# State and output of a chunked recurrence: two products of 40 and 64 columns per head joined into one of 104

## The chip, the cores and the metric

One core of one Trainium2 chip runs the whole program. The metric is device time in microseconds (us), the median of several executions; lower is better. PE below is TensorE, DVE VectorE, ACT ScalarE, POOL GpSimd, SP SyncE, which only issues transfers here.

## What is computed

The reference is a recurrence over 768 tokens for 4 batches of 8 heads of width 40, followed by two dense layers. Cut to the part that the change touches:

```python
for t in range(S):
    y[:, :, t] = np.einsum('bhd,bhde->bhe', rt, state)
    Sa = np.einsum('bhde,bhe->bhd', state, at)
    state_decay = state * wt[:, :, None, :] - np.einsum('bhd,bhe->bhde', Sa, bt)
    state = state_decay + np.einsum('bhd,bhe->bhde', vt, kt)
...
x = _moe_ref(x=y in token order, **moe_kwargs)   # 320 -> 2048 -> 320, with a sigmoid gate
return _moe2_ref(x=x, **moe2_kwargs)              # 320 -> 2 x 1536 -> 320, silu(gate) * value
```

## The kernel before

The recurrence is cut into 12 steps of 64 tokens (n = 0 to 11). Per step, `prepare` makes decays, scaled keys and a triangular inverse (`late`, from step 5 on, as 62 small DVE operations; `pieces` before that), and `advance` carries the state on. All 32 batch-heads are worked at once: 16 slots i, each holding two heads in partition halves. Products of 64 by 64 use one quarter of PE's array each; the loops run over k, r and p so that four neighbours in the program use four different quarters.

In `advance`, `w_one` and `w_two` make w from v, nk and the state `mt`; `u_mm` turns w into u (copied by ACT in `u_out`). Then:

- State: `m_one` (L1098, `tok0` times `v`) and `m_two` (`tok1` times `u`), 32 products of 40 columns each, summed in a PSUM bank; DVE adds the old state (`m_add`) and scales it (`m_scale`). `d_mm` transposes the state into `md`.
- Output: `ut_mm` transposes u; `scores` (L1227) makes `sv` from `vt` and `r`, and `su` from `ut` and `r`, masked by DVE. `y_old` (L1161) applies the old state in two phases with a drain between, `y_one` and `y_mm` (L1175) add `tok0` times `sv` and `tok1` times `su`, 32 products of 64 columns each. `y_out` scales the result, and `give` sends it by DMA to `xm`, from which the dense layer's input is built.

So `tok0` and `tok1` are each loaded as weights twice per step, once for 40 columns and once for 64.

The first dense layer (`Up`) runs between the pieces of the recurrence: 96 parts h (L495, 8 products of 512 columns, 2 steps of input per 16 parts) and 96 parts o (L522 to L529). The class `Plan` sets the order of everything on every engine at build time: each task has a cost, a due time, data it reads and writes; the recurrence has early due times, the dense parts the last (1e6). Where PE would stand without work, where too little work stood in a stretch before, or where a block of 256 PE instructions would be entered too early, the planner puts in fillers, `warm` (L453, one product of 512 columns of zeros, here called h<-still). The order is fixed; an engine that waits for one task holds all that stands behind it. After the last step the rest of the dense layer runs alone (the tail), then the second layer (`Down`).

```python
        if n + 1 < NT:
            plan.add("PE", 2.6 if 0 < n < self.EARLY else 1.25, m_one, ("v", "tok0", "mt"), ("m.p",), due + 0.005, bank=bm,
            plan.add("PE", 1.25, m_two, ("u", "tok1"), ("m.p",), due + 0.02, bank=bm, work=2200)
```

Of the kernel before, what the change touches and what calls it, by code (L numbers as in the profile page):

```python
# [6 lines left out]
F32 = mybir.dt.float32  # L7
# [5 lines left out]
ALU = mybir.AluOpType  # L13
# [4 lines left out]
B, H, S, D = 4, 8, 768, 40  # L18
DM = H * D
NSTEP = 6  # L20
T = 64
# [551 lines left out]
class Attention:  # L573
# [3 lines left out]
    def __init__(self, tc, ctx, cst, src, up):  # L577
# [32 lines left out]
        self.w = one.tile([128, 16, D], F32, name="w")  # L610
        self.u = one.tile([128, 16, T], F32, name="u")
        self.sv = one.tile([128, 2, H, T], F32, name="sv")
        self.su = one.tile([128, 2, H, T], F32, name="su")
        self.mt = one.tile([104, 2, 4, 2, T], F32, name="mt")
# [19 lines left out]
        v.memset(self.cend, 1.0)  # L634
        nc.gpsimd.memset(self.u, 0.0)
        nc.gpsimd.memset(self.mt, 0.0)
# [20 lines left out]
    def prepare(self, plan, n, due):  # L657
# [365 lines left out]
    def advance(self, plan, n, due):  # L1023

        nc = self.nc
        a, c = self.a[n % 2], self.c[n % 2]
# [32 lines left out]
        plan.add(("ACT",), (0.74,), w_out, ("w.p",), ("w",), due, bank=bw)  # L1059

        def u_mm():
# [9 lines left out]
        def u_out(e):  # L1071
            self.copy(e, self.u.rearrange("q (r k) d -> q r k d", r=2)[:, :, :, 0:D],
                      self.ps[bu.slot][:, :, 0:8 * D].rearrange("q r (k d) -> q r k d", d=D))

        tt = ("ttl", "tt0", "tt0.0", "tt1")
        middle = plan.add("PE", 1.25, u_mm, ("w",) + tt, ("u.p",), due + 0.01, bank=bu, into=("u",))
        plan.add(("ACT",), (0.74,), u_out, ("u.p",), ("u",), due + 0.01, bank=bu)

        def ut_mm():
            ps = self.ps[bx.slot]  # L1080
            for h in range(H):
                nc.tensor.transpose(
                    ps[:, h // 4, 128 * (h % 4):128 * (h % 4) + 128], self.u[:, 2 * h:2 * h + 2].rearrange("q z d -> q (z d)"), self.ident
                )
# [29 lines left out]
        def m_two():  # L1114
            m_part(1, self.u[:, :, 0:D])

# [16 lines left out]

        if n + 1 < NT:
            plan.add("PE", 2.6 if 0 < n < self.EARLY else 1.25, m_one, ("v", "tok0", "mt"), ("m.p",), due + 0.005, bank=bm,
                     work=4300 if 0 < n < self.EARLY else 2200, after=(middle,),
                     size=137 if 0 < n < self.EARLY else 128, real=2.5 if 0 < n < self.EARLY else 1.1)
            plan.add("PE", 1.25, m_two, ("u", "tok1"), ("m.p",), due + 0.02, bank=bm, work=2200)
# [5 lines left out]
        plan.add("PE", 0.9, ut_mm, ("u",), ("ut.p",), due + 0.03, bank=bx, into=("ut",))  # L1144
        plan.add(("ACT",), (1.05,), ut_out, ("ut.p",), ("ut",), due + 0.03, bank=bx)

        for src, dst, keys, d in ((self.vt, self.sv, ("vt", "sv"), -0.2), (self.ut, self.su, ("ut", "su"), 0.04)):
            marks = self.scores(plan, src, dst, keys, due + d)

        by = self.bank()  # L1150
# [15 lines left out]
        def y_part(j, x):  # L1166
            ps = self.ps[by.slot]
            l = self.tok[j].rearrange("q i e -> q (i e)")
            for k in range(8):
                for r in range(2):  # L1170
                    for p in range(2):
                        g, z = divmod(k, 2)
                        o, m = D * (8 * r + k), D if r else 64
                        s = slice(64 * p, 64 * p + 64)
                        nc.tensor.matmul(  # L1175
                            ps[64 * r:64 * r + m, p, T * k:T * k + T], l[s, o:o + m], x[s, z, 4 * r + g],
                            start=(n == 0 and j == 0 and k == 0), stop=(j == 1), skip_group_check=True,
                        )
# [12 lines left out]
        def y_out():  # L1191
            x = self.su[0:104].rearrange("q z h t -> q (z h t)").rearrange("q (k p t) -> q p k t", k=8, p=2)
# [5 lines left out]
        plan.add("PE", 1.25, y_one, ("tok0", "sv"), ("y.p",), due + 0.045, bank=by, work=2100, after=(marks,))  # L1198
        plan.add("PE", 1.25, y_mm, ("tok1", "su"), ("y.p",), due + 0.05, bank=by, into=("su",),
                 work=2500)  # L1200
        plan.add("DVE", 1.26, y_out, ("y.p", ck), ("su",), due + 0.05, bank=by, port=False)

# [15 lines left out]
    def scores(self, plan, src, dst, keys, due):  # L1218
# [13 lines left out]
        def out():  # L1232
            nc.vector.tensor_tensor(
                dst.rearrange("q z h t -> q (z h) t"), self.ps[b.slot].rearrange("q z (h t) -> q (z h) t", t=T),
                self.mask.unsqueeze(1).to_broadcast([128, 16, T]), op=ALU.mult,
            )
# [5 lines left out]
    def give(self, plan, n, due):  # L1242

        nc, t = self.nc, self.xm
        x = self.su.rearrange("q z h t -> q (z h t)").rearrange("q (g c) -> q g c", g=4)
        moves = []
# [6 lines left out]
        for i, (o, s, k) in enumerate(moves):  # L1253
            e, q, cost = ("ACT", nc.scalar, 0.76) if k == "xm1" else ("SP", nc.sync, 0.5)
            plan.add(e, cost, lambda o=o, s=s, q=q: q.dma_start(out=o, in_=s), ("su",), (f"{k}.{i}",), due, kb=80)
        m, half = divmod(n, 2)
# [585 lines left out]
```

## Time and profile before

| | us |
|---|---|
| median of 3 executions | 1117.69 |
| lowest, highest | 1112.75, 1117.75 |
| the profiled execution | 1112.34 |
| its span, first to last instruction | 1110.5 |
| PE busy in the span | 1073.1 (97%) |
| DVE busy | 702.2 (63%) |
| ACT busy | 436.0 (39%) |

In the profile a row of the timeline has a start, a duration from the first start to the last end, the engine, the line, the operation and a count. A 32-bit product of the program is two matrix instructions in the trace, so 32 products read x64. Durations of neighbours on PE overlap, so what a group costs is the start of the next group less its own start.

### The profile page before, as it was taken

To read this page: it belongs to the slowest core of one execution; us is meant where nothing else is said; L and a number is where in the kernel's file an instruction comes from. 1 tells how busy PE (TensorE), PEld (TensorE's weight loads), DVE (VectorE), ACT (ScalarE), POOL (GpSimd) and SP (SyncE) were. 2 spreads that over 40 slices of the span, in tenths; PEclk is the share of its full clock that TensorE was granted. 3 is DMA by queue.
4 is the path that set the end of the run, shared out by engine and by line. 5 is a ranking of instruction groups with operands and counts; after the bars stand their busy time and mean duration, and the time that the engine had idled before them with its cause. 6 is when DMAs were issued, how large, how long until landed. Compare 5 with 4: busy or idle time off the path is not lost.

```text
span 1110.5 us, 38519 instructions
## 1 busy us (share of the span) xinstructions
PE 1073.1 (97%) x16682; PEld 892.6 (80%) x16682; DVE 702.2 (63%) x1406; ACT 436.0 (39%) x814; POOL 98.2 (9%) x115
## 2 busy tenths in 40 slices
PE   8999999899999999999999999999999999999987
PEld 7777777678778787888788878888888888888876
DVE  8976797989697887979653667643443343443221
ACT  3443646454343534344343656432222222222221
POOL 0131123320100000000000323210000000000000
PEclk9896999999999999999999999999999999999999
DMA  6265547664353543544224677430423434341000
GB/s 209 73 184 171 180 150 219 180 195 140 113 166 111 161 133 103 162 127 137 87 62 131 201 212 228 142 90 1 141 69 115 124 116 126 96 147 59 24 1 27
DMA packets 141011, 141.88 MB, mean 128 GB/s; under 512 B 16032, under 2 KB 131744, under 8 KB 140832
## 3 DMA queue, kind: packets, MB, share of 16 engines
q1 hardware_dynamic: 134784, 131.48, 39.1%
q10 hardware_dynamic: 6048, 7.86, 2.1%
q8 instruction: 132, 2.16, 0.8%
q14 instruction: 47, 0.39, 0.1%
HBM read 118.04 MB, written 13.11 MB: 118 GB/s over the span
## 4 chain that ended last, share of the span: by engine, by line
PE 87%; DVE 5%; issue 3%; DMA 2%; ACT 1%; SPq 1%; ACTq 0%; POOL 0%; DVEq 0%
PE gv L1456 24%; PE h L495 15%; PE sums L527 4%; PE oacc L1477 4%; PE oacc L1476 4%; PE oacc L1475 4%; PE sums L528 3%; PE sums L529 3%; PE h L453 3%; PE ps L1175 2%; PE sums L523 2%; PE ps L1098 2%; PE sums L522 2%; PE ps L1227 2%; PE ps L740 1%
## 5 line engine op out<-in xcount | busy, mean ns | idle before, releaser
L1456 PE MATMUL gv<-xst,wg 128*128 128x512 f32 x1152 | 279.9, 395 | 0.0
L1456 PEld LDWEIGHTS gv<-xst,wg 128*128 128x128 f32 x1152 | 213.4, 188 | 45.7
L495 PE MATMUL h<-xst,wi 120*128 120x512 f32 x768 | 197.1, 398 | 0.0
L1461 DVE TENSOR_TENSOR sg<-gv,sg 128x512 f32<-128x512 f32 x72 | 49.8, 692 | 186.5 <-PE gv L1456 184.4
L495 PEld LDWEIGHTS h<-xst,wi 120*128 120x128 f32 x768 | 140.5, 188 | 30.6
L503 ACT ACTIVATE sg<-h 128x512 f32<-128x512 f32 x96 | 57.2, 596 | 152.6 <-PE h L495 145.0
L1462 ACT ACTIVATE gh<-sg 128x512 fp32r<-128x512 f32 x72 | 45.5, 632 | 143.0 <-DVE sg L1461 143.0
L510 DVE TENSOR_TENSOR gl<-sg,gh 128x512 fp32r<-128x512 f32 x90 | 63.4, 704 | 60.2 <-ACT gh L509 60.0
L1460 ACT ACTIVATE sg<-gv 128x512 f32<-128x512 f32 x72 | 43.0, 597 | 136.6 <-PE gv L1456 136.6
L323 POOL TENSOR_TENSOR cvw<-cvu,cva 128x256 uint32<-128x256 uint32 (+2 forms) x89 | 71.6, 805 | 274.1 <-DVE cvu L315 168.5
L1476 PE MATMUL oacc<-wo,gh 128*128 128x320 f32 x288 | 89.0, 309 | 0.0
L1477 PE MATMUL oacc<-wo,gl 128*128 128x320 f32 x288 | 89.0, 309 | 0.0
L1475 PE MATMUL oacc<-wo,gh 128*128 128x320 f32 x288 | 89.0, 309 | 0.0
L527 PE MATMUL sums<-gh,wo 128*128 128x512 f32 x192 | 80.8, 421 | 2.9 <-DVE sg L557 2.6
L1463 DVE TENSOR_TENSOR gl<-sg,gh 128x512 fp32r<-128x512 f32 x72 | 49.9, 692 | 50.2 <-ACT gh L1462 50.2
L528 PE MATMUL sums<-gh,wo 128*128 128x512 f32 x192 | 75.5, 393 | 0.0
L529 PE MATMUL sums<-gl,wo 128*128 128x512 f32 x192 | 75.2, 392 | 0.0
L509 ACT ACTIVATE gh<-sg 128x512 fp32r<-128x512 f32 x96 | 60.7, 632 | 3.6 <-ACT sg L503 0.3
L788 DVE TENSOR_TENSOR tsol<-tsol,tmp 128x126 f32<-128x126 f32 (+22 forms) x217 | 56.3, 260 | 6.7
L780 DVE TENSOR_TENSOR tmp<-tsol,nsol 128x126 f32<-128x126 f32 (+22 forms) x217 | 55.8, 257 | 6.9
L453 PE MATMUL h<-still 128*128 128x512 f32 x183 | 58.3, 466 | 1.1 <-DVE still L412 1.1
L1476 PEld LDWEIGHTS oacc<-wo,gh 128*128 128x128 f32 x288 | 54.1, 188 | 3.2
(182 smaller groups left out, 1618.8 us busy)
## 6 DMA issues: line engine op xcount, KB each, us to landing
wo<-w_out SPq DMA_DIRECT2D x192, 160.0 KB
cva<-out SPq DMA_DIRECT2D x128, 128.0 KB
cva<-gv SPq DMA_DIRECT2D x96, 128.0 KB
kb<-kba SPq DMA_DIRECT2D x92, 104.0 KB
cva<-in_ab SPq DMA_DIRECT2D x64, 120.0 KB
r<-rT SPq DMA_DIRECT2D x48, 104.0 KB
vt<-vT SPq DMA_DIRECT2D x48, 104.0 KB
a<-kba SPq DMA_DIRECT2D x46, 104.0 KB
```

Of the source, the lines that this page charges most:

```text
L323: nc.gpsimd.tensor_tensor(w.bitcast(U32), u, lo, op=ALU.add)
L453: self.nc.tensor.matmul(self.ph[0], c.to_broadcast([128, 128]), c.to_broadcast([128, 512]), start=True, stop=True)
L495: nc.tensor.matmul(ps[:, 0:n], self.wi[:, b, 128 * f:128 * f + 128], x[:, a], start=(e == 0), stop=(e == 7))
L509: add("ACT", 0.63, lambda: nc.scalar.activation(out=hi, in_=sg, func=ACTF.Copy), (f"sg{s}",), (f"gh{d}",))
L510: add(("DVE", "POOL"), (0.74, 1.35), lambda e: self.engine(e).tensor_tensor(lo, sg, hi.bitcast(F32), op=ALU.subtract), (f"sg{s}", f"gh{d}" ...
L527: nc.tensor.matmul(acc[k], w[:, c:c + 128], hi, start=st, stop=False)
L528: nc.tensor.matmul(acc[k], w[:, 256 + c:384 + c], hi, start=False, stop=False)
L529: nc.tensor.matmul(acc[k], w[:, c:c + 128], lo, start=False, stop=sp)
L1456: nc.tensor.matmul(ps, w[:, b], x[:, a], start=(i == 0), stop=(i == 7))
L1475: nc.tensor.matmul(acc[k], hi[:, c], self.wo[:, f, 0], start=st, stop=False)
L1476: nc.tensor.matmul(acc[k], hi[:, c], self.wo[:, f, 1], start=False, stop=False)
L1477: nc.tensor.matmul(acc[k], lo[:, c], self.wo[:, f, 0], start=False, stop=sp)
```

## The change

From step 5 on (`paired`), the state and the output of one head share a product. `v` and `sv` become the two parts of one tile `vs` (16 slots of 40 + 64 columns), `u` and `su` those of `us`. One product of 104 columns with `tok0` or `tok1` then gives both results. Because 104 columns times 8 slots don't fit a bank, the work is done in two halves f of four slots, each in a bank of its own: `pair_old` (the old state's share, with a drain in each half), `pair_mm` with `vs`, `pair_mm` with `us`, then `pair_add` and `pair_out` by DVE, and one `m_scale`. In step 11, which has no next state, only the 64 columns are computed. Before step 5 the products stay apart.

With it go: u is copied by ACT first into `nk` (read by the transposes and, before step 5, by `m_two`), and from step 5 on a second time into `us`; so nk of the next step can't be written before these readers are done. The output is written to `utr` in place of `su`. The mask of `scores` writes rows 104 apart. The load of v writes 40 columns of each 104, in pieces of 160 bytes in place of 640.

```diff
-        self.v = one.tile([128, 16, D], F32, name="v")
+        self.vs = one.tile([128, 16, D + T], F32, name="vs")
+        self.us = one.tile([128, 16, D + T], F32, name="us")
...
+        self.v, self.u = self.vs[:, :, 0:D], self.us[:, :, 0:D]
+        self.sv, self.su = self.vs[:, :, D:D + T], self.us[:, :, D:D + T]
...
-        load(self.v.rearrange("q i d -> q (i d)"), self.vtok[n], "v", 328, 0.6)
+        load(self.v, self.vtok[n].rearrange("q (i d) -> q i d", d=D), "v", 328, 0.6)
...
+        middle = plan.add("PE", 1.25, u_mm, ("w",) + tt, ("u.p",), due + 0.01, bank=bu, into=("nk",))
+        plan.add(("ACT",), (0.74,), lambda e: u_out(e, False), ("u.p",), ("nk",), due + 0.01, bank=bu)
+        if paired:
+            plan.add(("ACT",), (0.74,), lambda e: u_out(e, True), ("u.p",), ("u",), due + 0.01, bank=bu)
...
-        if n + 1 < NT:
+        if not paired and n + 1 < NT:
...
+        def pair_old(b, f):
+            ps = self.ps[b.slot]
+            md = self.md.rearrange("q i r e -> q (i r e)")
+            for ph in (1, 0):
+                if not ph:
+                    nc.tensor.drain()
+                for g in (2 * f, 2 * f + 1):
...
+        def pair_mm(b, f, j, x):
+            ps = self.ps[b.slot]
+            l = self.tok[j].rearrange("q i e -> q (i e)")
+            c = 0 if n + 1 < NT else D
+            for k in range(4):
+                for r in range(2):
+                    for p in range(2):
+                        i = 8 * r + 4 * f + k
+                        s, m = slice(64 * p, 64 * p + 64), D if r else 64
+                        nc.tensor.matmul(
+                            ps[64 * r:64 * r + m, p, W * k + c:W * k + W], l[s, D * i:D * i + m], x[s, i, c:W],
+                            start=False, stop=(j == 1), skip_group_check=True,
+                        )
...
+        if paired:
+            for f in range(2):
+                b = self.bank()
+                yk = (f"y.p{f}",)
+                plan.add("PE", 0.8, lambda b=b, f=f: pair_old(b, f), ("md", "r"), yk, due + 0.045, bank=b,
+                         work=1250, after=(marks,), size=65, real=0.75)
+                plan.add("PE", 0.85, lambda b=b, f=f: pair_mm(b, f, 0, self.vs), ("tok0", "v", "sv"), yk,
+                         due + 0.045, bank=b, work=1600, size=64, real=0.7)
+                plan.add("PE", 0.85, lambda b=b, f=f: pair_mm(b, f, 1, self.us), ("tok1", "u", "su"), yk,
+                         due + 0.05, bank=b, work=1600, size=64, real=0.7)
...
-        if n:
+        if n and not paired:
             plan.add("PE", 1.25, y_old, ("md", "r"), ("y.p",), due + 0.045, bank=by, work=2200, after=(marks,), size=129)
```

The planner makes a new order of it. On PE the fillers go from 183 to 211: from 178 to 185 ahead of the first dense part, from 5 (groups of 4 and 1) to 26 behind it (six groups of 3, one of 4, one of 2, two of 1). The dense layer is interrupted 91 times by work of the recurrence in place of 99. The last step's `w_two` stands behind 64 parts h in both orders.

The first place is PE in step 0, where the inverse of step 0 ends (L956, L965) and L995 is `nk_mm` of step 1. Before:

```order
L740 MATMUL sums<-kb,a_126 32x64 x4
L453 MATMUL h<-still 128x512 x5
L956 MATMUL ps_122<-tt,nb_139 32x32 x32
L995 MATMUL ps_123<-a_126,kb 64x64 x32
L453 MATMUL h<-still 128x512 x4
L965 MATMUL sums<-q,tn 32x32 x32
L453 MATMUL h<-still 128x512 x9
L1067 MATMUL ps_122<-w,tt 64x40 x32
```

And after:

```order
L740 MATMUL sums<-kb,a_126 32x64 x4
L453 MATMUL h<-still 128x512 x5
L956 MATMUL ps_122<-tt,nb_140 32x32 x32
L453 MATMUL h<-still 128x512 x10
L965 MATMUL ps_123<-q,tn 32x32 x32
L453 MATMUL h<-still 128x512 x9
L1069 MATMUL sums<-w,tt 64x40 x32
```

`nk_mm` of step 1 has left this place (it now stands after the key transposes of step 1), and six more fillers stand in it.

The second place is PE in a step from 5 on, at the transposes of u (L1082, after L1086) and `nb_mm` of the next step (L740, 64 products in 16 rows, of which the first two stand here). Before:

```order
L1098 MATMUL ps_123<-u,tok_137 64x40 x2
L1098 MATMUL ps_123<-u,tok_137 40x40 x2
L1082 MATMUL ps_122<-cst,u 128x128 x8
L495 MATMUL h<-xst_93,wi 128x512 x8
L740 MATMUL ps_123<-kb,a_126 32x32 x4
L740 MATMUL ps_123<-kb,a_126 32x64 x4
```

And after:

```order
L522 MATMUL sums<-gh_100,wo_105 128x512
L1086 MATMUL ps_122<-cst,nk 128x128 x8
L453 MATMUL h<-still 128x512 x3
L740 MATMUL ps_123<-kb,a_126 32x32 x4
L740 MATMUL ps_123<-kb,a_126 32x64 x4
L495 MATMUL h<-xst_94,wi 128x512 x8
```

The 40-column products are gone from here, and three fillers stand between the transposes and `nb_mm` where a dense part stood.

The third place is PE at the output products of such a step (rows that alternate between 64 and 40 weights repeat; the first two of each stand here). Before:

```order
L495 MATMUL h<-xst_93,wi 128x512 x8
L1161 MATMUL ps_123<-r,md 64x64 x2
L1161 MATMUL ps_123<-r,md 40x64 x2
L1175 MATMUL ps_123<-sv,tok_136 64x64 x2
L1175 MATMUL ps_123<-sv,tok_136 40x64 x2
L527 MATMUL sums<-gh_101,wo_105 128x512
L1175 MATMUL ps_123<-su,tok_137 64x64 x2
L1175 MATMUL ps_123<-su,tok_137 40x64 x2
L1207 MATMUL ps_122<-cst,mt 104x104 x8
```

And after:

```order
L1166 MATMUL ps_123<-r,md 64x64 x2
L1180 MATMUL ps_123<-vs,tok_137 64x104 x2
L1180 MATMUL ps_123<-vs,tok_137 40x104 x2
L527 MATMUL sums<-gh_101,wo_106 128x512
L1166 MATMUL ps_122<-r,md 64x64 x2
L1180 MATMUL ps_122<-vs,tok_137 64x104 x2
L1180 MATMUL ps_123<-us,tok_138 64x104 x2
L1180 MATMUL ps_122<-us,tok_138 64x104 x2
L495 MATMUL h<-xst_94,wi 128x512 x8
L1012 MATMUL ps_123<-cst,kb 128x104 x8
```

Three runs of products became six, of half as many products each, those of `pair_mm` with 104 columns.

## Rows read from the trace of the kernel before

**Rows 1.** The page, busy time, share of the span and instructions.

```profile
PE 1073.1 (97%) x16682; PEld 892.6 (80%) x16682; DVE 702.2 (63%) x1406; ACT 436.0 (39%) x814; POOL 98.2 (9%) x115
```

**Rows 2.** Busy time by stage; columns after PEld: DVE, ACT, POOL, clock, DMA.

```profile
0.00:125.00 125.00, 112.90 (x3061) 90.92 (x3065) 100.94 (x166) 49.83 (x102) 20.50 (x31) 0.88 0.52 157
125.00:592.00 467.00, 453.92 (x11138) 368.63 (x11128) 370.26 (x789) 211.69 (x376) 43.78 (x40) 1.00 0.47 142
592.00:702.00 110.00, 107.44 (x475) 87.51 (x467) 72.94 (x155) 65.96 (x144) 27.20 (x36) 1.00 0.67 201
```

**Rows 3.** Waits of PE from 120 us on: for what, us, times, longest.

```profile
PE sums L527 <- DVE sg L557: 2.6, 1, 2.6
PE ps L1098 <- issue: 1.9, 2, 1.7
```

**Rows 4.** Timeline of PE in step 10: start, us, engine, line, operation, count.

```profile
530.05 0.50 PE L527 MATMUL sums<-gh,wo 128*128 128x512 f32 x1
530.38 0.39 PE L528 MATMUL sums<-gh,wo 128*128 128x512 f32 x1
...
531.77 0.39 PE L522 MATMUL sums<-gh,wo 128*128 128x512 f32 x1
532.09 1.07 PE L1098 MATMUL ps<-v,tok 64*64 64x40 f32 x62
...
533.00 1.15 PE L1098 MATMUL ps<-u,tok 64*40 64x40 f32 x62
534.09 1.09 PE L1082 MATMUL ps<-cst,u 128*128 128x128 f32 x8
534.93 2.07 PE L495 MATMUL h<-xst,wi 120*128 120x512 f32 x8
...
541.33 1.45 PE L1161 MATMUL ps<-r,md 40*64 40x64 f32 x64
542.71 2.11 PE L495 MATMUL h<-xst,wi 120*128 120x512 f32 x8
544.74 1.15 PE L1175 MATMUL ps<-sv,tok 64*64 64x64 f32 x64
545.68 1.14 PE L1175 MATMUL ps<-su,tok 64*40 64x64 f32 x64
546.76 0.93 PE L1207 MATMUL ps<-cst,mt 104*104 104x104 f32 x8
```

**Rows 5.** Timeline of PE near the end of the start: groups of fillers.

```profile
105.33 0.48 PE L453 MATMUL h<-still 128*128 128x512 f32 x1
105.74 1.49 PE L1161 MATMUL ps<-r,md 40*64 40x64 f32 x64
...
108.09 0.92 PE L453 MATMUL h<-still 128*128 128x512 f32 x3
108.94 1.50 PE L1175 MATMUL ps<-su,tok 64*64 64x64 f32 x64
```

**Rows 6.** Timeline of PE at the first place of the order.

```profile
44.71 1.16 PE L995 MATMUL ps<-a,kb 40*64 40x64 f32 x64
45.80 1.97 PE L453 MATMUL h<-still 128*128 128x512 f32 x4
47.71 1.92 PE L965 MATMUL sums<-q,tn 32*32 32x32 f32 x64
```

**Rows 7.** Busy time around that place, with the granted clock (columns as in rows 2).

```profile
42.50:45.90 3.40, 2.26 (x127) 2.04 (x119) 3.12 (x9) 2.58 (x6) 1.35 (x2) 1.00 0.37 106
45.90:52.70 6.80, 6.80 (x75) 5.26 (x76) 6.46 (x14) 2.96 (x7) 0.00 (x0) 0.50 0.03 10
```

**Rows 8.** Waits of PE ahead of 125 us.

```profile
PE ps L917 <- issue: 1.9, 1, 1.9
PE ps L1098 <- issue: 1.7, 1, 1.7
```

**Rows 9.** Timeline of SP's queue, the load of v and what stands behind it.

```profile
430.55 2.37 SPq L670 DMA_DIRECT2D v<-vtok  x4
432.98 1.84 SPq L485 DMA_DIRECT2D wo<-w_out  x4
```

More of the change, by code (lines that the diff above doesn't have):

```diff
@@ new lines, in pair_mm @@
+        def pair_mm(b, f, j, x):
[3 more added lines that the diff above has]
+            for k in range(4):
+                for r in range(2):
+                    for p in range(2):
+                        i = 8 * r + 4 * f + k
+                        s, m = slice(64 * p, 64 * p + 64), D if r else 64
+                        nc.tensor.matmul(
+                            ps[64 * r:64 * r + m, p, W * k + c:W * k + W], l[s, D * i:D * i + m], x[s, i, c:W],
+                            start=False, stop=(j == 1), skip_group_check=True,
+                        )
@@ new lines, in pair_view, with pair_add, pair_out @@
+        def pair_view(b):
+            return self.ps[b.slot][0:104, :, 0:4 * W].rearrange("q p (k x) -> q p k x", x=W)
+        def pair_add(b, f):
+            x = mt[:, :, 4 * f:4 * f + 4]
+            nc.vector.tensor_tensor(x, pair_view(b)[:, :, :, 0:D], x, op=ALU.add)
+        def pair_out(b, f):
+            x = self.utr.rearrange("q h p t -> q (h p t)").rearrange("q (k p t) -> q p k t", k=8, p=2)
+            ct = c.rearrange("q (k p) x -> q p k x", p=2)[:, :, :, 0:T]
+            k = slice(4 * f, 4 * f + 4)
+            nc.vector.tensor_tensor(x[:, :, k], pair_view(b)[:, :, :, D:W], ct[:, :, k], op=ALU.mult)
@@ new lines, in advance @@
+        if paired:
[8 more added lines that the diff above has]
+                         due + 0.05, bank=b, work=1600, size=64, real=0.7)
+                if n + 1 < NT:
+                    plan.add("DVE", 0.5, lambda b=b, f=f: pair_add(b, f), yk + ("mt",), (f"mt.{f}",), due + 0.05,
+                             bank=b, port=False)
+                plan.add("DVE", 0.65, lambda b=b, f=f: pair_out(b, f), yk + (ck,) + (("ut.0",) if f else ()), ("ut",) if f else ("ut.0",),
+                         due + 0.05, bank=b, port=False, into=("ut",))
+            if n + 1 < NT:
+                plan.add("DVE", 0.9, m_scale, ("mt.0", "mt.1", ck), ("mt",), due + 0.05)
@@ L1191, in y_out @@
         def y_out():
-            x = self.su[0:104].rearrange("q z h t -> q (z h t)").rearrange("q (k p t) -> q p k t", k=8, p=2)
+            x = self.utr.rearrange("q h p t -> q (h p t)").rearrange("q (k p t) -> q p k t", k=8, p=2)
             ct = c.rearrange("q (k p) x -> q p k x", p=2)[:, :, :, 0:T]
             nc.vector.tensor_tensor(x, self.ps[by.slot][0:104].rearrange("q p (k t) -> q p k t", t=T), ct, op=ALU.mult)
-        if n:
+        if n and not paired:
             plan.add("PE", 1.25, y_old, ("md", "r"), ("y.p",), due + 0.045, bank=by, work=2200, after=(marks,), size=129)
[L1198 to L1201, printed above, removed]
+        if not paired:
+            plan.add("PE", 1.25, y_one, ("tok0", "sv"), ("y.p",), due + 0.045, bank=by, work=2100, after=(marks,))
+            plan.add("PE", 1.25, y_mm, ("tok1", "su"), ("y.p",), due + 0.05, bank=by,
+                     work=2500)
+            plan.add("DVE", 1.26, y_out, ("y.p", ck), ("ut",), due + 0.05, bank=by, port=False)
         def d_mm():
@@ L1244, in give @@
         nc, t = self.nc, self.xm
-        x = self.su.rearrange("q z h t -> q (z h t)").rearrange("q (g c) -> q g c", g=4)
+        x = self.utr.rearrange("q h p t -> q (h p t)").rearrange("q (g c) -> q g c", g=4)
         moves = []
@@ L1254, in give @@
             e, q, cost = ("ACT", nc.scalar, 0.76) if k == "xm1" else ("SP", nc.sync, 0.5)
-            plan.add(e, cost, lambda o=o, s=s, q=q: q.dma_start(out=o, in_=s), ("su",), (f"{k}.{i}",), due, kb=80)
+            plan.add(e, cost, lambda o=o, s=s, q=q: q.dma_start(out=o, in_=s), ("ut",), (f"{k}.{i}",), due, kb=80)
         m, half = divmod(n, 2)
```

34 lines of the change are left out of this document (17 added, 17 removed).

## The prediction, made before the changed kernel ran

> **What bounds the kernel now.** I read the page's busy times first. PE is busy 97% of the span, no other engine comes near [rows 1]. By stages the picture is sharper: in the first 125 us, where only the recurrence runs, PE is busy 112.9 of 125 us, but much of that is fillers and the clock is 0.88 on the mean; from 125 to 592 us, with the dense layer between the steps, PE is busy 453.9 of 467 us at full clock, and the tail after it 107.4 of 110 [rows 2]. The list of waits for that time names two that matter, 2.6 us in the tail and 1.9 us in the instruction stream [rows 3]. So from 125 us on PE's own work sets the end. The recurrence there is not late: the tail of 110 us is dense work left over when the last step is done. A longer chain inside a step therefore costs nothing as long as PE has dense parts in between, and a us of PE work removed or added in steps 5 to 11 moves the end by a us. That is the account that I make. In the start it is different: there the chain through DVE, ACT and PE counts, and fillers only count where they delay the next task.
>
> **The products.** In the timeline of a late step the two state products take 532.09 to 534.09, 2.00 us for 128 instructions; the old state's share takes 541.33 to 542.71, 1.38 us; the two output products 544.74 to 546.76, 2.02 us [rows 4]. Forty columns cost 15.6 ns each and sixty-four 15.8: the narrow ones pay a floor, and that is what the change can win. Steps 5 to 10 now cost 5.40 us each, step 11 (no state) 3.40, together 35.8 us.
>
> After the change: the old share without its drain would be like one output product, 1.01 us, so the drain is 0.37. A half is 0.50 + 0.37 = 0.87 us; 14 of them are 12.2. For 104 columns no row exists. Eight transposes of 128 columns take 534.09 to 534.93, 105 ns each [rows 4], so one quarter of the array would need 52 ns for 64 columns and 85 for 104. With four quarters at once that is 13.1 and 21.3 ns; the measured 15.8 is 2.7 above the first, so I take 21.3 + 2.7 = 24.0 ns, 0.77 us for a half of 32 instructions. 24 such halves are 18.5 us, step 11 with four halves of 64 columns 2.0. Sum 32.7: **3.1 us saved**. The bounds: if 104 columns still hide under the floor, a half is 0.51 and 9.4 us are saved; if only two quarters work at once (42.7 + 2.7 = 45 ns), a half is 1.45 and 13 us are lost. I take the middle since 64 columns already lie close to the four-quarter rate.
>
> Forty columns costing as much as sixty-four is also what the Trainium skill says, TensorEngine Tiling (Array Packing), section Instruction Overhead: a product of 1 column takes as long as one of 60. Taken by its count, 60 + 64 columns become 104, so the products of a step would fall by 20/124 of 4.02, or 0.65 us, where the rows give 0.94; the whole sum would come out 1.7 us higher by it.
>
> **The fillers.** The order shows 26 fillers after the first dense part where 5 stood. They stand mostly between the transposes of u and `nb_mm`, where PE is not short of dense work but has the next block of instructions to enter. A group of three costs 108.09 to 108.94, 0.85 us, a single one 0.41 [rows 5]. At 0.28 each, 21 more are **5.9 us added**. If PE would wait there for instructions anyway, their price is zero; so 0 to 5.9, and I take the upper end because the before kernel shows no such wait at this place in the seven late steps.
>
> **Interruptions.** Each change from dense products to quarter products costs a little: 531.77 to 532.09 is 0.32 where neighbours are 0.23 apart, and on the way back 530.05 to 530.38 is 0.33 [rows 4]. Eight interruptions fewer are 8 x 0.2 = 1.6 us; some of them are now towards transposes or fillers, so I take **1.0 saved** (0 to 1.6).
>
> **The start.** `nk_mm` of step 1 with four fillers took 44.71 to 47.71, 3.0 us [rows 6]. Now ten fillers stand there. The clock had fallen to 0.50 at 45.9 after a stretch in which PE was busy 2.26 of 3.40 us [rows 7]; at that clock a filler is 1.91/4 = 0.48 us, ten are 4.8, and all behind comes 1.8 us later. At full clock ten are about 2.5, and the work would come 0.5 earlier, or more if what follows also ran at full clock. `nk_mm` itself moves to step 1's key transposes, where it takes the place of fillers. I take **0.8 added** (-3 to +2).
>
> **What costs nothing.** DVE's two larger operations are cut into four and ACT copies u a second time, seven times each; DVE is busy 370 and ACT 212 of 467 us in that stage [rows 2], and on neither do the dense parts wait longer than their lag of two parts. nk and `utr` are held longer, the state is ready later in its step; PE works on dense parts meanwhile. If that cover were gone, PE would stand for the latency of one masked score, some 2 to 3 us a step.
>
> Sum: -3.1 + 5.9 - 1.0 + 0.8 = **+2.6 us** against the profiled execution's 1112.3, so 1114.9. The four executions shown lie at 1112.3, 1112.8, 1117.7 and 1117.8 (mean 1115.1, median of the three reported 1117.7), a spread that the change has no reason to end. I put the forecast at the mean plus the sum, **1117.7 us**. A measurement here can tell about 0.5%, 5.6 us, from no change.
>
> **The rivals.** *Instructions come too late (slower).* `nb_mm` is 64 short products, 256 instructions in 1.4 us, and now stands right behind other short work in place of a dense part. If the fillers don't bridge the fetch, PE waits at each of seven places as it did in the start, 1.9 and 1.7 us [rows 8]: 7 x 1.5 = 10 us more, 1128. It decides from 0.4 us of wait a place. For it speaks that such waits exist; against it that a step now issues 64 products fewer. Chance 0.17.
>
> *Two quarters at once (slower).* 13 us lost in place of 3 saved: 1134. Against it: 64 columns run near the four-quarter rate. Chance 0.06.
>
> *The floor hides 104 columns, and the fillers only fill waits (faster).* 9.4 saved, 1.0 saved, fillers 0 to 2, start 0: about 1106 to 1108. For it: no rise from 40 to 64 columns. Against it: 85/4 is above 15.8. Chance 0.17.
>
> *The load of v comes late (slower).* Its pieces are 160 bytes, and it can now start only behind the wide products. It is issued in 2.4 us with the dense layer's weights behind it on SP's queue [rows 9]. Were it four times as long, 10 us a load, it would still land before `w_one` of the next step, which stands five dense parts later, some 25 us; it decides only beyond that, and would then cost 3 us a step, 1135. Chance 0.03. The Trainium skill, DMA: Bandwidth & Descriptors, section Specifications, asks for at least 512 bytes a transfer for full rate, which speaks against these pieces; no run here shows yet what 160 bytes cost.
>
> *The gain is put back by the order* is no rival but the forecast itself: the planner spends on fillers what the products save. Chance of the forecast 0.57.
>
> **How the numbers follow.** The forecast's own range is 1112 to 1123 (the two groups of executions, and the terms' inner bounds). With the faster rival inside and the instruction rival at the edge the range is 1107 to 1128; outside lie the two dear rivals and the ends. Faster by over 0.5% 0.18, within 0.5% 0.56, slower by over 0.5% 0.26.
>
> **What would show it.** In the changed kernel the runs at L1180 should start 0.77 us apart (0.51 or 1.45 by the rivals) and L1166 0.87. Fillers at L453 after the first dense part should be 26, groups of three 0.85 us long. The waits of PE on the instruction stream at L740 should stay under 0.4 us, the tail should still be some 110 us, and L1036 should wait for no transfer. The prediction is wrong if L1180 is far from 0.77, if PE waits at L740, or if the first dense part starts more than 3 us from where it did.

## The result, and the profile after

The changed kernel takes 1129.99 us (median of 6 executions, 1126.50 to 1135.09); the kernel before took 1115.15 on the same chip (6 executions, 1112.75 to 1117.75). The ratio is 1.0138, with a 95% interval of 1.0107 to 1.0168: about 15 us slower, where 0.5% (5.6 us) can be told from no change. The forecast was 1117.7 us, its range 1107 to 1128. The profiled execution took 1129.89 us, its span 1128.1; it stands 17.6 us above that of before (1112.34), a little more than the medians do. Ratios and intervals leave out the few executions that lie over 1.5% above the fastest of the same kernel (further down two of f3, and one of the kernel before beside i1 to i3).

The page's busy times after, which answer to [rows 1]:

```profile
PE 1077.1 (95%) x15942; PEld 895.5 (79%) x15942; DVE 700.2 (62%) x1420; ACT 439.1 (39%) x821; POOL 91.9 (8%) x114
```

740 matrix instructions are gone, and yet PE is busy 4 us longer and stands idle 13.6 us longer (span less busy time: 51.0 against 37.4 us). So the loss isn't work alone. The stages say where it is. First before, with the middle stage of [rows 2] cut at 290 us, near step 5 (its `w_two` starts at 271.0 us before and at 286.5 after), and the last stage ended where `Down` begins (701.7 us); columns are the stretch, its length, the busy times of PE, PEld, DVE, ACT and POOL, the granted clock, the DMA share and GB/s:

```profile
125.00:290.00 165.00, 156.02 (x4321) 124.93 (x4319) 136.05 (x257) 88.50 (x172) 35.84 (x35) 1.00 0.60 181
290.00:592.00 302.00, 297.89 (x6833) 243.70 (x6832) 234.21 (x532) 123.19 (x204) 7.94 (x5) 1.00 0.40 121
592.00:701.70 109.70, 107.14 (x473) 87.28 (x465) 72.64 (x154) 65.68 (x143) 27.20 (x36) 1.00 0.67 201
```

The same after, where `Down` begins at 718.6 us:

```profile
0.00:125.00 125.00, 109.44 (x3091) 89.28 (x3091) 104.44 (x177) 51.74 (x108) 21.39 (x30) 0.94 0.57 166
125.00:290.00 165.00, 153.23 (x4093) 122.43 (x4092) 128.03 (x243) 82.92 (x162) 28.79 (x34) 0.98 0.56 166
290.00:592.00 302.00, 293.71 (x5993) 238.80 (x5986) 233.46 (x545) 125.89 (x210) 6.44 (x5) 1.00 0.41 122
592.00:718.60 126.60, 120.09 (x754) 97.59 (x752) 76.71 (x163) 71.11 (x153) 29.09 (x38) 0.99 0.61 185
```

The first dense part starts at 125.0 us (before 125.5), and from the start of `Down` to the end of the span it is 408.8 us before and 409.5 after. All is lost between 125 us and `Down`, 17 us. To divide it, I take at each step the start of `w_two` and subtract 1.84 us for every dense part that PE has run by then (8 products, 0.23 apart, as in [rows 4]). What is left is the time that the recurrence, fillers and waits took. The table counts each part where it lies: "to step 5" includes the start.

| us, dense parts subtracted | before | after | |
|---|---|---|---|
| to `w_two` of step 5 | 212.1 | 220.2 | +8.1 |
| from there to `w_two` of step 11 | 127.9 | 130.9 | +3.0 |
| from there to the first product of `Down` | 12.0 | 17.9 | +5.9 |

So three places, and the joined products only lie in the middle one and in a little of the last. `t_mm` of step 5, the last product of its inverse (1.3 us), stands ahead of that `w_two` after and behind it before, so 1.3 us of the first row belong to the second. Some of what PE waited for up to 290 us before (what it waited for, us, times, longest):

```profile
PE ps L1098 <- issue: 3.6, 3, 1.7
PE ps L917 <- issue: 1.9, 1, 1.9
PE ps L1012 <- ACT md L647: 1.7, 1, 1.7
PE ps L740 <- DVE kb L714: 1.2, 1, 1.2
```

And after:

```profile
PE ps L1102 <- issue: 3.6, 3, 1.8
PE ps L1293 <- ACT tt L647: 2.7, 2, 1.9
PE ps L995 <- ACT tt L647: 2.5, 1, 2.5
PE ps L1227 <- DVE us L1299: 2.2, 1, 2.2
PE ps L1036 <- issue: 1.2, 1, 1.2
PE ps L1012 <- ACT q L647: 1.2, 1, 1.2
```

The waits on the instruction stream (issue) are alike. New are waits on ACT and DVE ahead of L995 (`nk_mm`), L1293 (`scores`), L1227 (the old state's share) and L1012 (the key transposes): 8.6 us, where the two such waits of before made 2.9. PE's idle time up to 290 us rose by 6.2 us (rows above and [rows 2]). The granted clock blurs this pair. Ahead of the first dense part it was 0.88 before and 0.94 after, which gave back some 7 us of full clock and hid waits there; behind it, up to 290 us, it was 1.00 before and 0.98 after, which cost 3. So the table shows the loss behind the first dense part alone, and some of it is clock; the profiles of the other kernels are needed to place it (they follow).

The timeline of a late step after (start, us, engine, line, operation, count), to hold against [rows 4]:

```profile
544.74 1.04 PE L1086 MATMUL ps<-cst,nk 128*128 128x128 f32 x8
545.58 0.92 PE L453 MATMUL h<-still 128*128 128x512 f32 x3
546.43 1.44 PE L740 MATMUL ps<-kb,a 40*32 40x32 f32 x128
547.81 0.50 PE L527 MATMUL sums<-gh,wo 128*128 128x512 f32 x1
...
550.83 0.98 PE L1166 MATMUL ps<-r,md 40*64 40x64 f32 x32
551.63 0.90 PE L1180 MATMUL ps<-vs,tok 64*40 64x104 f32 x32
552.45 2.11 PE L495 MATMUL h<-xst,wi 120*128 120x512 f32 x8
554.50 1.02 PE L1166 MATMUL ps<-r,md 40*64 40x64 f32 x32
555.34 0.90 PE L1180 MATMUL ps<-vs,tok 64*40 64x104 f32 x32
556.05 1.61 PE L1180 MATMUL ps<-us,tok 64*40 64x104 f32 x63
558.46 0.25 PE L1180 MATMUL ps<-us,tok 64*40 64x104 f32 x1 [0.80 <-issue]
558.63 0.50 PE L527 MATMUL sums<-gh,wo 128*128 128x512 f32 x1
```

A half of 104 columns takes 0.71 us (555.34 to 556.05), or 0.82 where a dense part follows; the old state's half 0.80 to 0.84; three fillers 0.85. All are close to what was worked out. Here one instruction came 0.80 us late; in 290 to 592 us there are two waits at L740 (1.8 us) and this one on the instruction stream.

The third place is the tail. PE and then ACT there, after:

```profile
701.82 0.39 PE L522 MATMUL sums<-gh,wo 128*128 128x512 f32 x1
705.87 3.22 PE L495 MATMUL h<-xst,wi 120*128 120x512 f32 x8 [3.66 <-ACT sg L503]
```

```profile
698.68 0.40 ACT L1435 ACTIVATE wg<-cvw 128x256 fp32r<-128x256 f32 x1
703.87 0.43 ACT L307 ACTIVATE cva<-cva 128x256 uint32<-128x256 uint32 x1 [4.79 <-DMA cva<-gv]
704.20 0.61 ACT L1503 ACTIVATE xst<-xr 128x512 fp32r<-128x512 f32 x1
704.72 0.61 ACT L1506 ACTIVATE xst<-xr 128x512 fp32r<-128x512 f32 x1
705.24 0.58 ACT L503 ACTIVATE sg<-h 128x512 f32<-128x512 f32 x1
```

ACT stands 4.79 us at a conversion of the second layer's weights, whose transfer hasn't landed; behind it in ACT's fixed order is the sigmoid (L503) of a part that PE had computed by 700.2 us, and PE waits 3.66 us for it. Behind that the granted clock is down (columns as in the stages above):

```profile
706.60:710.00 3.40, 3.40 (x10) 2.62 (x9) 2.87 (x7) 1.67 (x5) 0.74 (x1) 0.50 0.23 76
```

It is 0.50, the lower of its two levels (1.2 GHz), and the eight products of L495 take 3.0 us (705.87 to 708.89) in place of 1.84. In the tail of before, PE waits for no sigmoid [rows 3]. In the program, every part h whose last operation (DVE's or POOL's on its gated values) is left over for the tail asks there for eleven more pieces of weight conversion (`down.prepare(11)`). Such requests number 27 after, 26 before: the new order left one more.

### The profile page after: what moved, and what is told of

The parts are those of the page before. It is cut to its first block, busy times and chain, and to the rows that moved or that the text cites. A ratio compares the mean times of both kernels' runs of the same rounds, so it can differ in the third digit from the quotient of the medians.

```text
span 1128.1 us, 37066 instructions
## 1 busy us (share of the span) xinstructions
PE 1077.1 (95%) x15942; PEld 895.5 (79%) x15942; DVE 700.2 (62%) x1420; ACT 439.1 (39%) x821; POOL 91.9 (8%) x114
## 3 DMA queue, kind: packets, MB, share of 16 engines
q1 hardware_dynamic: 153216, 131.48, 39.3%
## 4 chain that ended last, share of the span: by engine, by line
PE 79%; DVE 7%; DMA 5%; issue 3%; ACT 2%; SPq 2%; ACTq 0%; POOL 0%; DVEq 0%; POOLq 0%
PE gv L1522 24%; PE h L495 14%; PE sums L527 4%; PE oacc L1543 4%; PE oacc L1541 4%; PE oacc L1542 4%; PE sums L528 3%; PE sums L529 3%; PE ps L1293 2%; PE sums L523 2%; PE ps L1180 2%; PE sums L522 2%; PE ps L740 1%; PE h L453 1%; PE ps L965 1%
## 5 line engine op out<-in xcount | busy, mean ns | idle before, releaser
L495 PE MATMUL h<-xst,wi 120*128 120x512 f32 x768 | 199.9, 403 | 3.7 <-ACT sg L503 3.7
L495 PEld LDWEIGHTS h<-xst,wi 120*128 120x128 f32 x768 | 142.4, 190 | 36.3 <-ACT sg L503 4.1
L503 ACT ACTIVATE sg<-h 128x512 f32<-128x512 f32 x96 | 57.2, 596 | 168.0 <-PE h L495 142.2
L510 DVE TENSOR_TENSOR gl<-sg,gh 128x512 fp32r<-128x512 f32 x86 | 59.9, 696 | 72.6 <-ACT gh L509 72.5
L323 POOL TENSOR_TENSOR cvw<-cvu,cva 128x256 uint32<-128x256 uint32 (+2 forms) x89 | 68.5, 771 | 269.8 <-DVE cvu L315 113.0
L1529 DVE TENSOR_TENSOR gl<-sg,gh 128x512 fp32r<-128x512 f32 x72 | 49.8, 692 | 50.2 <-ACT gh L1528 50.2
L453 PE MATMUL h<-still 128*128 128x512 f32 x211 | 60.8, 427 | 1.2 <-DVE still L412 1.0
```

What stands on the lines that cost most here:

```text
L323: nc.gpsimd.tensor_tensor(w.bitcast(U32), u, lo, op=ALU.add)
L453: self.nc.tensor.matmul(self.ph[0], c.to_broadcast([128, 128]), c.to_broadcast([128, 512]), start=True, stop=True)
L495: nc.tensor.matmul(ps[:, 0:n], self.wi[:, b, 128 * f:128 * f + 128], x[:, a], start=(e == 0), stop=(e == 7))
L510: add(("DVE", "POOL"), (0.74, 1.35), lambda e: self.engine(e).tensor_tensor(lo, sg, hi.bitcast(F32), op=ALU.subtract), (f"sg{s}", f"gh{d}" ...
```

## The experiments

Three parts of the change could each be the loss: the joined products with their fillers; nk, held longer because u is first copied into it (this gives the new order of the start); and the tail's extra request. The kernel before took 1121 to 1124 us on the chips that were used here, with a wider spread of executions than on the first one (1113 to 1132), so kernels of one group are compared with each other, and ratios are to the kernel before on the same chip.

**All of the change but the joining.**

```diff
-        paired = n >= self.EARLY
+        paired = False
```

> The changed kernel with all its new tiles and keys (u copied into nk, output in utr, v in pieces of 160 bytes), but with the products of 40 and 64 columns left apart in every step; up to step 5 its PE order is that of the changed kernel. Theory A (holding nk for u, and the order that follows, makes steps 0 to 4 some 8 us longer): the non-dense time up to the w_two of step 5 stays at about 220 us, the late steps fall back to about 128 us, the time is 1121 to 1128. Theory B (the joined products themselves cost the 15 us): 1115, as before. Theory C (the pieces of 160 bytes slow the early transfers): like A here, the next kernels tell them apart.

Measured 1128.20 us, ratio 1.0035 (1.0003 to 1.0067). To step 5 the account gives 224.5 us, from there to step 11 131.5, the tail 12.7. The start is late without a single joined product.

**u in a tile of its own.** u is first copied to a new tile `uw`, read by the transposes and `m_two`, and nk is free as before; to make room, w lies in the first columns of `su`. PE's order up to step 5 is then that of before.

```diff
-            self.copy(e, (self.us if whole else self.nk)[:, :, 0:D].rearrange("q (r k) d -> q r k d", r=2),
+            self.copy(e, (self.us if whole else self.uw)[:, :, 0:D].rearrange("q (r k) d -> q r k d", r=2),
...
+        self.w = self.us[:, :, D:D + D]
```

> The changed kernel with the joined products, but u has a tile of its own again and nk is not held (w lies in the unused columns of us to make room); up to step 5 its PE order is that of the kernel before. Theory A: the early 8 us are gone, late steps cost about 3 us more than before, the tail 0 to 5: 1117 to 1123. Theory B or C: no better than the changed kernel, 1128 to 1132.

Measured 1131.60 us, 1.0092 (1.0067 to 1.0117). The time to step 5 falls to 217.5 us and the new waits on ACT's `tt` are gone, but 29 requests now lie in the tail: it takes 17.5 us, 4.6 of them a wait for the sigmoid. One cost was taken away and another made larger; that pointed to the tail.

**The late fillers left out.** The order of all else is kept, and the 26 fillers behind the first dense part are not run.

```diff
     for t in order:
-        if t.begin <= end:
+        if t.begin <= end and not (t.due == 2e6 and t.begin > first):
             t.run()
```

> The changed kernel with its order kept and the 26 fillers after the first dense part left out. If fillers are pure cost: about 5.5 us less, 1124. If they stand where PE would wait for instructions: the waits on issue at L740 grow by as much, and the time stays at 1130.

Measured 1126.47 us, 1.0026 (1.0000 to 1.0052). From step 5 to 11 the account gives 128.6 us in place of 130.9. The changed kernel was not timed beside it; that comes with i1.

**v in short pieces.** The kernel before, with v's load alone split into 160-byte pieces:

```diff
-        load(self.v.rearrange("q i d -> q (i d)"), self.vtok[n], "v", 328, 0.6)
+        for i in range(4):
+            r, c = i // 2, slice(4 * (i % 2), 4 * (i % 2) + 4)
+            nc.sync.dma_start(out=self.v[:, 8 * r + c.start:8 * r + c.stop], in_=s[:, r, c])
```

> The kernel before, with the load of v alone changed: read in pieces of 160 bytes in place of 640 (the slots lie in another order in the input and are put right by the transfer). Theory A: 1115, no change. Theory C: 1120 to 1125, and w_one or the start waits for transfers.

Measured 1121.37 us, 1.0014 (0.9989 to 1.0039): not to be told from nothing. The pages show the packets, before and then in e4:

```profile
DMA packets 141011, 141.88 MB, mean 128 GB/s; under 512 B 16032, under 2 KB 131744, under 8 KB 140832
DMA packets 159443, 141.88 MB, mean 127 GB/s; under 512 B 40608, under 2 KB 150176, under 8 KB 159264
```

**The tail's request, taken away.** f1 is the changed kernel itself on that chip. f2 leaves out the first of its 27 requests; f3 is e2 with 26 requests in place of 29; f4 is f3 without the 17 fillers from step 5 on (the edit of e3, with step 5's `w_two` for `first`).

```diff
                         if hasattr(t, "last"):
-                            down.prepare(11)
+                            if skip:
+                                skip -= 1
+                            else:
+                                down.prepare(11)
```

> The changed kernel as it is, timed on the same chip as the next three. Both theories: slower than before by 10 to 15 us.

> The changed kernel with one change in the tail: the first of the 27 dense parts there doesn't ask for the next weights' conversion, so that 26 do, as before. If the tail's 5 us are an effect of where that work stands: no wait of the dense products on ACT there, 3 to 5 us less than the changed kernel. If the wait came from elsewhere (later data of the last steps): no change.

> u in a tile of its own (so nk isn't held) and the tail's requests brought back to 26 from the 29 that this order leaves: the products stay joined. If early order and tail carry the loss: 2 to 5 us over before. If the joining itself costs: still 10 us over before.

> As the one ahead, and without the 17 fillers from step 5 on. If those are pure cost: 4 us below the one ahead, thus level with before or some 2 us faster. If they hold the clock or bridge the instruction stream: no better than the one ahead, with more waits on issue or dips of the granted clock in steps 5 to 11.

Measured: f1 1131.71 us, 1.0097 (1.0062 to 1.0133); f2 1130.49, 1.0080 (1.0048 to 1.0112); f3 1127.31 (1125.45 with the two left out), 1.0029 (0.9994 to 1.0064); f4 1129.65, 1.0090 (1.0054 to 1.0125). In f2 the wait for the sigmoid is gone from the tail (0.2 us, the tail 14.7 in place of f1's 17.3), but the medians differ by 1.2 us, less than the intervals can tell. With both side costs taken off, f3 has most of the loss back. f4 was a surprise: without fillers it was not faster. Its windows show stretches of low clock; the columns are those above:

```profile
295.80:299.20 3.40, 2.07 (x66) 1.77 (x67) 3.13 (x7) 1.05 (x2) 0.00 (x0) 0.90 0.04 8
299.20:302.60 3.40, 3.40 (x36) 2.37 (x38) 1.36 (x6) 0.35 (x1) 0.00 (x0) 0.60 0.00 0
...
520.20:523.60 3.40, 1.80 (x109) 1.72 (x108) 3.40 (x5) 2.32 (x4) 0.00 (x0) 1.00 0.56 170
523.60:527.00 3.40, 3.40 (x43) 2.74 (x36) 3.33 (x4) 0.66 (x2) 0.00 (x0) 0.53 0.03 8
```

After stretches in which PE was busy 2.07 and 1.80 of 3.40 us the granted clock falls to 0.60 and 0.53. It does so three times between 290 and 592 us; in f3, with its fillers, not once. That is no proof that the fillers hold the clock, since profiles of kernels with all their fillers have such stretches there too: g4, the same kernel as f3, down to 0.70, and the changed kernel in f2 (0.73) and in h3:

```profile
418.20:421.60 3.40, 1.86 (x64) 1.79 (x64) 2.64 (x8) 3.19 (x7) 0.00 (x0) 0.74 0.81 245
421.60:425.00 3.40, 3.40 (x14) 2.48 (x8) 3.16 (x12) 0.44 (x2) 0.00 (x0) 0.50 0.52 166
```

What made f4 slow stays open.

**One part at a time, from the kernel before.** g1 is f3 with its products apart, the new tiles alone; g4 is f3 again. g2 changes only where u lies; g3 only adds one request ahead of the tail.

```diff
-            self.copy(e, self.u.rearrange("q (r k) d -> q r k d", r=2)[:, :, :, 0:D],
+            self.copy(e, self.nk[:, :, 0:D].rearrange("q (r k) d -> q r k d", r=2),
```

```diff
                     parts = iter(())
+                    down.prepare(11)
                     for t in tail:
```

> The kernel of f3_own_u_tail with the products kept apart in every step: u in a tile of its own, w in columns of us, v read in 160-byte pieces, 26 tail requests, and no product of 104 columns. It is the before kernel in all but the tiles. Theory (the held buffer and the tail request cost, the joining about +2 us): level with the before kernel, 1.000, within 0.003 of it. Rival (the new tiles themselves cost: two-stride operands of 104 columns a row on PE, ACT and DVE): 1.005 or more. Its distance to g4_joined_again is the price of the joining alone: by the theory +2 us (products -3.5, fillers +5.9, interruptions -1), by the rival that the joining is the loss +10 us.

> The before kernel with one edit: u_out writes u into the first 40 columns of nk, and the transposes and m_two read it there, so that nk of the next step can't be written before they are done. No products joined, tail requests 26 as before. Theory (the held buffer moves nk_mm of the next step behind its key transposes in the fixed order of PE, and the start pays): step 5's w_two, less the dense parts ahead of it, 5 to 10 us later than before (212 us there), waits of PE on ACT's copy of tt and of q ahead of 290 us, and a ratio of 1.004 to 1.009. Rival (nk held costs nothing, as the prediction had it; the start of the changed kernel is late for the tiles or the fillers): ratio 1.000, step 5 within 2 us of before.

> The before kernel with one more request for the next weights' conversion at the head of the tail, 27 in place of 26, nothing else. Theory (one request too many fills ACT and DVE at the wrong place, and PE waits for the gate in the tail): a wait of L495 on ACT's sg of 2 to 4 us appears in the tail, time ahead of it as before, and the ratio is 1.002 to 1.004. Rival (the tail is late in the changed kernel for another reason, such as which parts are left): no such wait, ratio 1.000.

> The kernel of f3_own_u_tail once more, beside its unjoined sister g1: products of 104 columns from step five, u in a tile of its own, 26 tail requests. Theory: 2 us above g1 (products -3.5, interruptions -1, fillers +5.9), ratio to the before kernel 1.002. Rival (the joining is the loss): 10 us above g1, ratio 1.009.

Measured: g1 1120.98 us, 0.9969 (0.9935 to 1.0002); g2 1125.72, 1.0018 (0.9993 to 1.0044); g3 1127.36, 1.0050 (1.0016 to 1.0084); g4 1125.28, 1.0032 (1.0003 to 1.0061).

The new tiles cost nothing. Joining alone, g4 over g1, is 4.3 us slower by the medians and 7 us by the ratios (0.0063; their intervals allow 2 to 12 us): between the +2 us of the theory and the rival's +10, and not a gain. In g2 `w_two` of step 5 stands at 217.9 us by the account, 5.8 later than before, as expected, but the ratio is lower than expected and not told from 1. g2's order on PE in the start is that of the changed kernel, and waits that the kernel before doesn't have are there (its list of PE's waits up to 290 us):

```profile
PE ps L1012 <- DVE su L1194: 3.1, 1, 3.1
...
PE ps L1161 <- DVE su L1233: 2.3, 1, 2.3
```

They are not the ones on `tt` that were expected: the same order holds PE up at other places. g3 shows the expected wait in the tail of a kernel that is otherwise unchanged:

```profile
PE h L495 <- ACT sg L503: 5.2, 2, 3.1
```

Its tail takes 20.6 us by the account, against 11.1 to 13.9 in the six profiles of kernels with products apart and 26 requests.

**Do they add up?** h1 is g2 and g3 together, h2 is g2 again, h3 the changed kernel.

> The before kernel with two edits and no joined products: u written into nk (as in g2_u_in_nk) and one more tail request (as in g3_tail_request). Theory (three separate costs that add up): 1.002 + 1.005 - 1, so 1.007, and the changed kernel h3_changed_again stands 4 us above it, by the price of the joining. Rival (the costs overlap, one of them hides in the other): 1.005 or below, the level of g3 alone.

> The kernel of g2_u_in_nk once more, since its interval there, 0.9993 to 1.0044, leaves open whether the held buffer costs at all. Theory: 1.002 to 1.005, and step 5 again later than before, by the time less the dense parts. Rival (nk held costs nothing): 1.000, interval around it.

> The changed kernel itself beside the two, on one chip. Theory: 1.010 to 1.014, as far above h1_nk_and_tail as g4_joined_again stood above g1_own_u_unjoined (4 us, 0.006 by the ratios). Rival (its loss is the buffer and the request alone): level with h1.

Measured: h1 1134.86 us, 1.0113 (1.0069 to 1.0156); h2 1128.21, 1.0041 (1.0011 to 1.0072); h3 1135.68, 1.0129 (1.0094 to 1.0165). The held buffer costs, by h2 now told from zero. Buffer and request together, with no product joined, make about as slow a kernel as the changed one, and a slower one than the 1.007 that was expected of them, though the interval still holds it. The 0.0016 between h1 and h3 leaves, with their intervals, -4 to 8 us for the joining.

**The fillers once more.** Across chips e3 spoke for their price, f4 against it. So i1 is e3's kernel beside the changed one, i2; i3 is i1 without the first tail request (the edit of f2).

> The kernel of e3_no_fillers once more, beside the changed kernel on one chip: the order of the changed kernel with the 26 fillers behind the first dense part left out. By the prediction's upper bound (each filler is 0.28 us of PE's time): 7 us below i2_changed_third, ratio to the kernel before 1.003. By its lower bound (fillers only fill waits, or give back the clock): level with i2, 1.010.

> The changed kernel as a control beside i1 and i3: 1.010 to 1.014.

> The changed kernel without the 26 late fillers and without the first of the 27 tail requests. If fillers and request each cost what the terms say: 7 + 5 us below i2_changed_third, ratio 1.000, the best that the joined products would give here. If the fillers cost nothing: 5 us below i2, 1.006.

Measured: i1 1128.68 us, 1.0021 (0.9989 to 1.0053); i2 1133.73, 1.0077 (1.0045 to 1.0109); i3 1127.26, 1.0044 (1.0015 to 1.0072). In the changed kernel the fillers cost 5.05 us by the medians, near the upper end that the prediction took. From step 5 to 11 i1 and i3 take 125.9 and 126.4 us, below every profile of a kernel with products apart (127.9 to 132.1); but e3, the same kernel as i1, took 128.6 and f4 133.9, so that the joined products gain without fillers is not shown. i3 is not faster than i1 beyond the intervals, so a request less gives back little in the changed kernel (1.4 us by the medians, and 1.2 in f2), though one more costs 6 us in the kernel before. No version was found that beats the kernel before: g1, i1 and f3 can't be told from it.

## Why the prediction was wrong

**The products: right.** Predicted were 35.8 us for steps 5 to 11 before and 32.7 after, 3.1 saved. Start to start, the state and output products with the old state's share took 36.2 before and 33.4 after: 2.8 saved with the 0.80 us wait of above in it, 3.6 without. A half of 104 columns was put at 0.77 us; the twelve with `vs` take 0.72 where another product of the recurrence follows and 0.83 where a dense part does, 0.76 on the mean. Neither rival on this point came: a floor that hides 104 columns would give 0.51, two quarters at once 1.45. Forty and sixty-four columns cost 15.6 and 15.8 ns [rows 4], 104 cost 22.5 (0.72 us for 32), so columns begin to count between 64 and 104. The Trainium skill, TensorEngine Tiling (Array Packing), section Instruction Overhead, counts everything up to 60 columns as 60. By its ratio 104 would cost, as an estimate, 104/60 x 15.7 = 27 ns; the trace has 22.5, and decides.

**The fillers: right in sum.** Start to start, fillers between 125 us and `Down` took 1.5 us before and 7.4 after, the 5.9 that were predicted. i1 beside i2 gives 5.05 us for leaving them out. f4 speaks against that price: without 17 of them it was slower than f3, by 0.0061. Why it is so in f4 and not in i1, runs can't say.

**Interruptions: right; step 5 to 11 as a whole: too low.** What the dense parts took beyond 1.84 us each fell by 1.4 us between `w_two` of step 5 and that of step 11 (65 runs of them before, 56 after), where 1.0 was taken. The terms make -3.1 + 5.9 - 1.0 = +1.8 us for the joining. The account gives +3.0 (127.9 to 130.9), with `t_mm` counted alike 4.3; over all profiles of kernels with fillers, 133.0 on the mean of eight with joined products against 130.1 on the mean of eight without; g4 over g1 4 to 7. All above the term, by 1 to 5 us. What was left out is the handful of waits on the instruction stream at L740 and L1180 (0.7 to 1.1 us each), 2.6 us in the profile after. That was the rival "instructions come too late": it came at three places, not seven, and the sum gave it nothing; the bound that was set for L740, 0.4 us a wait, is broken (1.1).

**The start: wrong.** The step that failed put `nk_mm` and ten fillers at +0.8 us (-3 to +2), since `nk_mm` "takes the place of fillers" at the key transposes of step 1, and "nk and `utr` are held longer ... PE works on dense parts meanwhile" at nothing. The account has +8.1 us there, 6.8 without `t_mm`. The ten fillers were no loss: they took 2.4 us (43.38 to 45.76). But `nk_mm` took the place of one filler: from `d_mm` of step 0 to `w_two` of step 1 PE runs 27 before and 26 after, and ahead of 125 us there is no dense part to cover for it. Its rows before and after (`d_mm` L1207 and L1273, `nk_mm` L995, `scores` L1293, `w_two` L1048):

```profile
58.98 0.88 PE L1207 MATMUL ps<-cst,mt 104*104 104x104 f32 x8
82.17 0.43 PE L1048 MATMUL ps<-mt,a 40*64 40x40 f32 x12
```

```profile
56.95 0.90 PE L1273 MATMUL sums<-cst,mt 104*104 104x104 f32 x8 [0.83 <-DVE mt L1134]
72.69 1.16 PE L995 MATMUL ps<-a,kb 40*64 40x64 f32 x64
75.72 1.26 PE L1293 MATMUL ps<-r,vt 40*64 40x64 f32 x64 [1.86 <-ACT tt L647]
85.66 2.14 PE L1048 MATMUL ps<-mt,a 40*64 40x40 f32 x64
```

That stretch takes 23.2 us before and 28.7 after, and the other profiles agree without overlap: 28.7 to 33.3 us in the twelve with nk held (mean 31.0), 23.2 to 27.9 in the eight with nk free (mean 25.2). `nk_mm` itself is about 1 us of it; the rest is waits, which lie at other places from kernel to kernel (here on ACT's `tt`, in g2 3.9 us on the instruction stream), and a lower granted clock (0.78 to 0.94 against 0.85 to 1.00). `nk_mm` of step 4 moved too, from ahead of the transposes of u of step 3 (194.69 us) to behind them (220.22); that of step 2 did not, and the 2.5 us wait at L995 in the list of after is its (121.69 us): the place is that of before, but ACT's copy of `tt` came late, queued behind a weight conversion that waited 1.62 us for its transfer.

"The first dense part within 3 us" held (125.0 against 125.5) by luck: it starts at 127.2 us on the mean of the nine profiles with nk held and the fillers left in, at 124.0 on that of the eight with nk free. The runs size the whole: g2 and h2, the held buffer alone, cost 2 to 5 us (1.0018 and 1.0041); to step 5 the same nine profiles (after, e1, f1, f2, g2, h1, h2, h3, i2) take 217.9 to 227.5 us, mean 222.1, and the eight (before, e2, e4, f3, f4, g1, g3, g4) 212.1 to 224.2, mean 217.1. Less the 1.3 us of `t_mm`, some 4 us of the 8 are the buffer's; the rest lies within what two profiles of one kernel differ by (f3 213.8, g4 224.2). The prediction's reading of [rows 3] had a hint: the same list has two more waits of that size, on ACT (1.7 us at L1012 and 1.6 at L995), so PE was not always covered behind 120 us either.

**The tail: not weighed at all.** "The tail still some 110 us" was a check, not a term. That the planner might leave other dense parts in it, and that some of them carry a request that fills ACT's queue, stood in the code and in the order, and the requests (26 to 27) could have been counted. The rows had a hint: [rows 2] show ACT busy 60% and the DMA share at 0.67 in that stage, the highest of the three. g3 shows what one request more does: 6.2 us by the medians, and the wait that the changed kernel has. All profiles agree on the wait: with 27 or 29 requests PE stands 2.2 to 5.2 us for the sigmoid in the tail, with 26 at most 0.6. How much the changed kernel would regain without the request is open, since f2 and i3 gave 1 to 2 us.

**What costs nothing: right for the load.** The 160-byte pieces of v left no trace (e4; g1 carries them too). The Trainium skill, DMA: Bandwidth & Descriptors, section Specifications, wants 512 bytes and more for full rate. The share of the main queue was 39.1% before, 40.1% in e4 and 39.3% after: packets that short cost a little of the queue here, and no time that can be told from none. DVE's halves and ACT's second copy cannot be told apart from the rest; between 290 and 592 us no wait of PE on either is longer than 1.4 us.

**The sum.** Buffer 2 to 5, request 6, joining 1 to 7, new tiles 0 to -3: 6 to 18, where 15 were measured on the first chip and 9 to 14 on the others (1.0077 to 1.0129). h1, buffer and request without the joining, gave 13 us where its parts make 8 to 11, so each of these sizes holds to some 3 us, and the share of the joining least of all. That buffer and request, the one put at nothing and the other not weighed, carry most of the loss is shown both ways: h1 has it without any joined product, and f3 and g4, with joined products but neither of the two, stand at 1.0029 and 1.0032. One of the prediction's sums does not come out: the rival of the hidden floor, 1117.7 us with its own terms, is 1104.7 to 1106.7, below the 1106 to 1108 that stand there and outside the range; nothing hung on it here.

## What to carry to other kernels

Where a planner or a fixed order decides, a change has two prices: the operations that it changes, and the order that follows from it. A buffer that is held longer can only be free where the engine has other work at that place: follow every moved instruction to the place where it lands, and ask what is queued ahead of it there. Count, too, what a part carries besides its own work: here one request more in the tail, put into the kernel before, cost 6 us, twice what the joined products saved.

## What was not expected of the hardware

Waits on the instruction stream stand at fixed places. Counted over PE's instructions in a profile (products, weight loads and its sequencer's), 311 of the 319 waits on issue of over 0.3 us ahead of 720 us, in all twenty profiles, stand at place 193 or 194 of a block of 256, counted from 0; not every block has one. A stall breeds another: behind the 3.66 us wait in the tail the clock was at 0.50 for 3.4 us, which cost 1.2 us more on one dense part. And 104 columns on a quarter of the array cost 22.5 ns, over 1.4 times as much as 64, while 40 cost as much as 64.
